# The last output projection of an RWKV5 and SwiGLU kernel: four of its thirds done unit by unit, stores of whole rows

## The chip, the cores and the metric

The kernel runs on one core of a Trainium2 chip. The metric is the device time of one execution in microseconds (us). The median of three runs before the change is 592.14 us (592.13 to 592.17).

## The reference

Two stages. The first is a linear attention with a decaying state (4 batches, 8 heads, 768 steps, head size 48); the second is a SwiGLU feed-forward block over the 3072 rows that come out of it.

```python
for t in range(S):
    cur = np.einsum('bhd,bhe->bhde', u[None] * kt, vt)
    y[:, :, t] = np.einsum('bhd,bhde->bhe', rt, state + cur)
    state = w[None, :, :, None] * state + np.einsum('bhd,bhe->bhde', kt, vt)
x = y.transpose(0, 2, 1, 3).reshape(B * S, H * D)      # 3072 x 384
g = x @ w_gate                                          # 384 x 1536
out = (g * (1.0 / (1.0 + np.exp(-g))) * (x @ w_val)) @ w_out   # 1536 x 384
```

All of it is in 32-bit floats. The change concerns only the last product, hidden values times `w_out`, for the last rows.

## The kernel before, in words

The 3072 rows are 24 blocks of 128 rows. Two blocks make a group for the feed-forward block, and from group 2 on two groups are worked on as a pair. A pair has two *units*, q = 0 and 1, with two blocks each, j = 0 and 1; so a pair puts out four blocks of 128 rows x 384 columns, 192 KB each. All engine orders are written out by hand: the program is a list of small pieces, and each engine does its instructions in the order in which the pieces issue them.

The output projections of the last two pairs use a product of matrices cut into thirds that takes 15 part products instead of 18. The function `project_thirds(g)` gives 15 pieces, one for each part product; here they are called *items* and go by the names r0 to r14 in the list `THIRDS`. An item multiplies a sum of hidden values by a sum of weights: for both units, four matmuls of 128x128x128 each, which are 16 matmul instructions on TensorE (PE). The result goes to a PSUM bank. Items of one *chain* (l1, l2, l8, n, y, l4, l5) add up in the same bank, and after each item the bank is evicted: copied, added or subtracted into one or two of the six output tiles c0 to c5 in SBUF, as the table `used` says. Copies are done by ScalarE (ACT), additions and subtractions by VectorE (DVE). Tile c[k] holds, for both units, 128 columns: block j = k % 2, third k // 2.

The items stand in this order; the second name is the chain:

```python
("r3", "l1"), ("r1", "l2"), ("r4", "l1"), ("r0", "l2"), ("r8", "l8"),
("r10", "n"), ("r14", "y"), ("r12", "l4"), ("r13", "n"), ("r2", "y"), ("r6", "l5"),
("r9", "l4"), ("r5", "n"), ("r11", "y"), ("r7", "l5"),
```

Before an item, `make(n)` may build sums of hidden values on DVE (line 999) that later items need. For the very last pair the flag `ends` is set.

PSUM has eight banks here: four in the queue `free` (the names bank0 to bank3) and four in `ring_a` (ring0 to ring3). A chain's first item takes a bank from the front of `free`; when the last item of a chain (`lasts`) has been evicted, the bank goes to the end of `free`. In the last projection chain l5 is *split*: it takes a second bank from `ring_a`, so that each unit has a bank of its own and is evicted as soon as its half of the item is done. The other chains hold both units in one bank, side by side, and are evicted for both at once with instructions of 128x256.

A block's row is whole when its three tiles are: block j = 0 with r9, r5 and r11, block j = 1 with r5, r11 and r7. So after r11 the blocks j = 0 of both units are stored in whole, and with `ends` also the first two thirds of the blocks j = 1 (128 KB each); the last third follows after r7 (64 KB each). Stores of unit 0 are issued by SyncE (SP), those of unit 1 by ACT, on the two engines' DMA queues q1 and q10. That makes six stores at the end of the kernel. For the pair before (`ends` not set) there are four whole stores, all issued by ACT.

The lines concerned: 999 (sums of hidden values), 1020 and 1022 (evictions by copy and by sum), 1027 (matmuls), 995 (stores); 944 to 951 prepare operands on GpSimd (POOL). After the last piece every engine takes a branch over a general version of the kernel that isn't run here (line 1381), and SP waits for all DMA semaphores.

Of the kernel before, what the change touches and what calls it, by code (L numbers as in the profile page):

```python
# [15 lines left out]
P = 128  # L16
# [6 lines left out]
def fast(  # L23
# [32 lines left out]
    DM, DFF = moe_w_gate.shape  # L56
# [8 lines left out]
    dve, pool, act, pe, sp = nc.vector, nc.gpsimd, nc.scalar, nc.tensor, nc.sync  # L65
# [23 lines left out]
    free = deque(banks[:2])  # L89

    ring_a = deque(ps_a.tile([P, 4 * P], FP32, name=f"ring{n}") for n in range(4))
# [6 lines left out]
    def take():  # L98
        return free.popleft()
# [178 lines left out]
    for e in range(2):  # L278
# [3 lines left out]
        out=u_row, in_=bass.AP(tensor=u.tensor, offset=u.offset, ap=[[0, 1], [1, H * D]]),  # L282
# [9 lines left out]
    def warm(n, bank=None):  # L292
# [14 lines left out]
        out=mask[:], in_=mask[:], compare_op=ALU.is_gt, fill=0.0,  # L307
# [11 lines left out]
    for l in range(7):  # L319
        n = 1 << l  # L320
# [451 lines left out]
    def prepare_threes(g, n):  # L772
        if n == 6:
            x_forms(g)
        for _ in range(2):
            if todo_x:
                todo_x.popleft()()
        if g > THREES:
            return
        if n == 1:  # L780
            if g == FIRST:
                todo_forms.extend(in_place(0) + in_place(1))
            if g == THREES:
                todo_forms.extend(w_forms(g, 1))
        if n == 7:
            todo_forms.extendleft(reversed(w_forms(g, 0)))
        for _ in range(2):
            if todo_forms:
                todo_forms.popleft()()
# [127 lines left out]
    def third(x, k, j):  # L917

        return x[:, :, 4 * k : 4 * k + 4, P * j : P * j + P]
# [39 lines left out]
    def project_thirds(g):  # L959

        ends = g + 2 == N // 2
        A, B_, C, D_, E, F = room["h"]
        (x00, x01), (x10, x11), (x20, x21) = (
            [third(hTs, k, j) for j in range(2)] for k in range(3)
        )
        h = {
            "r3": A, "r4": B_, "r1": C, "r0": D_, "r8": E, "r10": F, "r14": A, "r13": B_,
            "r12": C, "r2": D_, "r6": E, "r5": x00, "r7": x21, "r9": x20, "r11": x11,
        }
        rows = hv[:, NR + 6 : NR + 12].rearrange("p (q r) t -> p q (r t)", q=2)  # L970
        c = [rows[:, :, DM * (k % 2) + P * (k // 2) :][:, :, 0:P] for k in range(6)]
        made = {
            0: [(dve.tensor_sub, E, x01, x11)],
            1: [(dve.tensor_add, F, x01, x21)],
            2: [(dve.tensor_add, A, x10, x20)],
            3: [(dve.tensor_sub, B_, x00, F)],
            4: [(dve.tensor_add, C, B_, x20)],
            5: [(dve.tensor_sub, D_[q], D_[q], x20[:, q]) for q in range(2)],
            6: [(dve.tensor_add, E[:, q], D_[q], x21[:, q]) for q in range(2)],
        }  # L980
        used = {
            "r3": [("copy", 2)], "r4": [("copy", 1)], "r1": [("copy", 0)], "r0": [("sub", 2)],
            "r8": [("copy", 3), ("sub", 1)], "r10": [("copy", 5)], "r14": [("copy", 4)],
            "r12": [("add", 0)], "r13": [("add", 4)], "r2": [("add", 5)], "r6": [("add", 3)],
            "r9": [("sub", 4)], "r5": [("sub", 0), ("sub", 1)], "r11": [("add", 2), ("add", 3)],
            "r7": [("add", 5)],
        }
        lasts = ("r4", "r0", "r8", "r9", "r5", "r11", "r7")
        open_ = {}

        def store(q, j, a=0, z=DM):
            cc, b = divmod(2 * (g + q) + j, B)
            n0 = S * b + P * cc
            issue = sp if ends and q == 0 else act
            issue.dma_start(out=out[n0 : n0 + P, a:z], in_=rows[:, q, DM * j + a : DM * j + z])

        def make(n):
            for op, o, a, b in made.get(n, ()):
                op(o, a, b)
            if not ends:  # L1000
                prepare_threes(g + 2, n)

        def item(n):
            what, chain = THIRDS[n]
            if n:
                make(n)
            first = chain not in open_
            split = ends and chain == "l5"
            if first:
                open_[chain] = [take()] + ([ring_a.popleft()] if split else [])  # L1010
            banks_ = open_[chain]

            def evict(q):
                for how, k in used[what]:
                    x = banks_[0][:, 0 : 2 * P].rearrange("p (q t) -> p q t", q=2)
                    if split:
                        x = banks_[q][:, q * P : q * P + P]
                    o = c[k][:, q] if split else c[k]
                    if how == "copy":
                        act.copy(o, x)  # L1020
                    else:
                        (dve.tensor_add if how == "add" else dve.tensor_sub)(o, o, x)

            for q in range(2):
                ps = banks_[q if split else 0][:, q * P : q * P + P]
                for f in range(4):
                    pe.matmul(  # L1027
                        ps, (h[what][q] if h[what] is D_ else h[what][:, q])[:, f, :], wide["o"][what][:, f, :],
                        start=first and f == 0 and (split or q == 0), stop=f == 3, skip_group_check=True,
                    )  # L1030
                if split:
                    evict(q)
                    if what == "r7":
                        store(q, 1, 2 * P)
            if not split:
                evict(None)
            if n == 0:
                for do in wide.pop("last"):
                    do()
                make(0)  # L1040
            if what in lasts:
                free.append(banks_[0])
            if what == "r11":
                store(0, 0)
                store(1, 0)
                if ends:
                    store(0, 1, 0, 2 * P)
                    store(1, 1, 0, 2 * P)
            if what == "r7" and not ends:
                store(0, 1)  # L1050
                store(1, 1)
        return [lambda n=n: item(n) for n in range(15)]

    def three_units(g):
# [226 lines left out]
    for s in range(4, N + 2):  # L1281
# [3 lines left out]
        if s + 2 == SWAPPED:  # L1285
# [3 lines left out]
            for p, o in ((slice(0, 64), 64), (slice(64, P), -64)):  # L1289
                sp.dma_start(  # L1290
                    out=halves_of[p], in_=scales[p.start + o : p.stop + o, 1:3, H // 2 : H]
# [65 lines left out]
    ])  # L1357
    threes = three_units(THREES), three_units(THREES + 2)
    projections = project_thirds(THREES), project_thirds(THREES + 2)
    tail = threes[0] + projections[0][:-2]  # L1360
    tail += threes[1][0:1] + projections[0][-2:-1] + threes[1][1:2] + projections[0][-1:]
    tail += threes[1][2:] + projections[1]
    n = nc.values_load(outside, min_val=0, max_val=512)
# [416 lines left out]
```

## Time and profile before

| what | value |
|---|---|
| median of three runs | 592.14 us |
| the profiled execution | 591.4 us |
| its span | 589.7 us |
| PE busy | 578.3 us, 98% of the span |
| DVE busy | 421.0 us, 71% |
| ACT busy | 225.6 us, 38% |
| POOL busy | 355.5 us, 60% |
| granted TensorE clock | full in all 40 slices |
| stores at the end | 6: two of 192 KB, two of 128 KB, two of 64 KB |

The times in the traces are counted from the start of the span of one profiled execution. A line of the timeline gives start, duration, engine, source line, operation, and output <- inputs; "PEld" is TensorE's weight load, which runs beside its matmuls, and "SPq" and "ACTq" are the issuing of DMAs by these engines, not the transfer itself. The chain of waits is the work that ended last, followed back from the end. "To landing" is the time from a DMA's issue until its semaphore is complete.

### The profile page before, as it was taken

The numbers are of one execution on the slowest core, as the hardware profiler recorded it, in microseconds if no ns is written. First come the engines' busy times: TensorE is split into PE (matmuls) and PEld (weight loads), VectorE is DVE, ScalarE is ACT, GpSimd is POOL, SyncE is SP. The second block draws the span as 40 slices with busy tenths as digits, with TensorE's granted clock in tenths as the row PEclk, the third lists the DMA queues.
The fourth block names the chain that finished last, engine by engine and source line by source line (L and its number), as shares of the span: only waits on it lengthen the run. The fifth ranks groups of instructions, "written<-read, shape, count | busy, mean of one in ns | idle before, by whom it ended". The sixth has DMA issues, their size and how long they took to land.

```text
span 589.7 us, 13188 instructions
## 1 busy us (share of the span) xinstructions
PE 578.3 (98%) x5210; PEld 519.7 (88%) x5210; DVE 421.0 (71%) x703; ACT 225.6 (38%) x517; POOL 355.5 (60%) x378
## 2 busy tenths in 40 slices
PE   8999999999999999999999999999999999999996
PEld 7778888899888899988899988899988899888896
DVE  7788786479588776577887477779257877377672
ACT  4478885322343512245332345432134320233310
POOL 6899888989999403887501997422778960010610
PEclk9999999999999999999999999999999999999999
DMA  8989969432442323233244233200100000100001
GB/s 201 230 223 261 292 217 91 74 65 49 76 74 37 57 40 75 48 66 53 38 64 88 51 61 52 46 9 2 54 2 0 2 1 1 55 0 1 1 1 57
DMA packets 148292, 41.48 MB, mean 70 GB/s; under 512 B 138497, under 2 KB 142082, under 8 KB 148226
## 3 DMA queue, kind: packets, MB, share of 16 engines
q1 hardware_dynamic: 144914, 36.27, 30.4%
q10 hardware_dynamic: 3312, 4.33, 2.0%
q8 instruction: 42, 0.69, 0.5%
q14 instruction: 24, 0.20, 0.1%
HBM read 28.31 MB, written 4.72 MB: 56 GB/s over the span
## 4 chain that ended last, share of the span: by engine, by line
PE 93%; DVE 1%; ACT 0%; issue 0%; DVEq 0%; ACTq 0%
PE bank L801 31%; PE bank L620 18%; PE ring L801 13%; PE bank L545 10%; PE bank L1027 9%; PE ring L507 6%; PE ring L454 3%; PE ring L522 1%; PE ring L385 1%; DVE hv L825 0%; PE ring L1027 0%; DVE hs L594 0%; ACT At L364 0%; DVE hs L593 0%; DVE At L464 0%
## 5 line engine op out<-in xcount | busy, mean ns | idle before, releaser
L825 DVE TENSOR_TENSOR hv<-hv,bank 128x512 f32<-128x512 f32 x132 | 87.3, 681 | 26.3 <-PE bank L801 15.2
L545 PE MATMUL bank<-xT,wgv 128*128 128x256 f32 x288 | 66.2, 384 | 0.0
L801 PE MATMUL bank<-xf,wgv 128*128 128x256 f32 x256 | 65.9, 382 | 0.0
L364 ACT ACTIVATE At<-ident,du 128x128 f32<-128x128 f32 x176 | 59.9, 398 | 15.8 <-DVE du L265 8.9
L825 ACT COPY hv<-bank 128x512 f32<-128x512 f32 x72 | 40.1, 585 | 57.8 <-PE bank L801 51.4
L545 PEld LDWEIGHTS bank<-xT,wgv 128*128 128x128 f32 x288 | 53.4, 190 | 7.9
L731 POOL TENSOR_TENSOR s<-wgv 128x256 f32<-128x256 f32 x39 | 29.9, 790 | 48.6 <-PE bank L620 48.4
L801 PEld LDWEIGHTS bank<-xf,wgv 128*128 128x128 f32 x256 | 47.8, 190 | 7.0 <-DVE kT L1072 0.6
L1081 POOL TENSOR_TENSOR hv<-At,hats 128x512 f32<-128x512 f32 x8 | 10.2, 1277 | 66.3 <-ACT At L1080 66.3
L535 POOL TENSOR_TENSOR Z<-Z,w 48x192 f32<-48x192 f32 x32 | 16.8, 526 | 36.8 <-DVE Z L534 35.6
L507 PE MATMUL ring<-At,v_ld 128*32 128x128 f32 x768 | 35.6, 273 | 3.4 <-DVE At L464 2.5
L832 ACT ACTIVATE hv<-hv 128x512 f32<-128x512 f32 (+1 forms) x33 | 21.2, 668 | 45.4 <-DVE hv L825 45.3
L801 PE MATMUL bank<-xT,wgv 128*128 128x256 f32 x144 | 35.9, 382 | 0.0
L801 PE MATMUL bank<-xT,s 128*128 128x256 f32 x152 | 35.2, 380 | 0.0
L507 PEld LDWEIGHTS ring<-At,v_ld 128*32 128x32 f32 x768 | 30.5, 110 | 5.0 <-DVE At L464 4.5
L620 PE MATMUL bank<-wt,hs 128*128 128x192 f32 x192 | 33.7, 328 | 0.6 <-DVE hs L594 0.6
L620 PE MATMUL bank<-wo,hs 128*128 128x192 f32 x192 | 33.9, 327 | 0.0
L620 PE MATMUL bank<-wo,hv 128*128 128x192 f32 x192 | 33.4, 327 | 0.0
L801 PEld LDWEIGHTS bank<-xT,s 128*128 128x128 f32 x152 | 28.6, 190 | 4.5 <-issue 0.6
L620 PEld LDWEIGHTS bank<-wt,hs 128*128 128x128 f32 x192 | 31.3, 190 | 1.4 <-ACT At L364 0.8
L620 PEld LDWEIGHTS bank<-wo,hv 128*128 128x128 f32 x192 | 31.6, 190 | 0.4
L620 PEld LDWEIGHTS bank<-wo,hs 128*128 128x128 f32 x192 | 31.6, 190 | 0.3
(224 smaller groups left out, 1394.6 us busy)
## 6 DMA issues: line engine op xcount, KB each, us to landing
hats<-hats SPq DMA_DIRECT2D x192, 32.0 KB, 2.0
w_bits<-in_moe_w_gate_dram SPq DMA_DIRECT2D x6, 768.0 KB, 6.2
w_bits<-in_moe_w_val_dram SPq DMA_DIRECT2D x6, 768.0 KB, 6.2
w_bits<-in_moe_w_out_dram SPq DMA_DIRECT2D x6, 768.0 KB, 7.0
out_dram<-hv ACTq DMA_DIRECT2D x21, 192.0 KB, 1.9
v_ld<-in_v_dram SPq DMA_DIRECT2D x24, 96.0 KB, 5.5
k_ld<-in_k_dram SPq DMA_DIRECT2D x8, 192.0 KB, 4.3
r_ld<-in_r_dram SPq DMA_DIRECT2D x8, 192.0 KB, 4.4
```

What stands on the lines that cost most here:

```text
L364: lambda h=h: act.activation(At[i % 2][:, h, :], ident[:], AF.Identity, scale=du[:, h : h + 1])
L454: pe.matmul(ps[e][keys, a, cols], kT[i % 2][rows, at(i, a), keys], turned[i][rows, at(i, a), cols], start=True, stop=True, skip_group_chec ...
L507: pe.matmul(ps[32 * q : 32 * q + 32, cc, :], *x, start=start, stop=stop, skip_group_check=True,)
L535: pool.tensor_mul(ze, ze, w)
L545: pe.matmul(gv[:, o, :].rearrange("p (i t) -> p i t", i=2), wt[:, c, P * f : P * (f + 1)], xT[:, 2 * g % NX : 2 * g % NX + 2, c, :], start ...
L620: pe.matmul(ps, lhs[:, f, :], rhs[:, f, :], start=(f == 0 and n in (0, 1, 4)), stop=(f == FH - 1), skip_group_check=True,)
L731: op(made[o], made[a], made[b])
L801: pe.matmul(ps[:, o], u[:, o], v, start=first and o == 0, stop=True, skip_group_check=True,)
L825: do(out, *(pair_of(wide[a][:]) if isinstance(a, str) else a for a in args))
L832: todo.append((at, lambda: act.activation(gate, gate, AF.Silu)))
L1027: pe.matmul(ps, (h[what][q] if h[what] is D_ else h[what][:, q])[:, f, :], wide["o"][what][:, f, :], start=first and f == 0 and (split or ...
L1081: todo.append((muls, lambda: on.tensor_mul(h, sg, value)))
```

## The change

In the last pair the four last items (r9, r5, r11, r7) are done for unit 0 and then for unit 1, where they were done for both units each. For that, all four chains that these items belong to (n, y, l4, l5) are split: each unit has a bank of its own and evictions of 128x128. Both banks are taken when the chain opens, from `free`, or from `ring_a` when `free` is empty, and aren't given back. The six stores become four of whole rows: block 0 of a unit after its r11, block 1 after its r7. SP issues those of block 0 and ACT those of block 1. Other pairs are as before.

```diff
-        def store(q, j, a=0, z=DM):
+        def store(q, j):
...
-            issue = sp if ends and q == 0 else act
-            issue.dma_start(out=out[n0 : n0 + P, a:z], in_=rows[:, q, DM * j + a : DM * j + z])
+            issue = sp if ends and j == 0 else act
+            issue.dma_start(out=out[n0 : n0 + P, :], in_=rows[:, q, DM * j : DM * j + DM])
...
-        def item(n):
+        def item(n, halves=(0, 1)):
...
-            split = ends and chain == "l5"
+            split = ends and chain in ("n", "y", "l4", "l5")
             if first:
-                open_[chain] = [take()] + ([ring_a.popleft()] if split else [])
+                open_[chain] = [(free or ring_a).popleft() for _ in range(2 if split else 1)]
...
-            for q in range(2):
+            for q in halves:
...
                 if split:
                     evict(q)
-                    if what == "r7":
-                        store(q, 1, 2 * P)
+                    if what in ("r11", "r7"):
+                        store(q, what == "r7")
...
-            if what in lasts:
+            if what in lasts and not split:
                 free.append(banks_[0])
-            if what == "r11":
+            if what == "r11" and not ends:
                 store(0, 0)
                 store(1, 0)
-                if ends:
-                    store(0, 1, 0, 2 * P)
-                    store(1, 1, 0, 2 * P)
             if what == "r7" and not ends:
                 store(0, 1)
                 store(1, 1)
+        if ends:
+            pieces = [lambda n=n: item(n) for n in range(11)]
+            return pieces + [lambda n=n, q=q: item(n, (q,)) for q in range(2) for n in range(11, 15)]
         return [lambda n=n: item(n) for n in range(15)]
```

## The prediction

> **What bounds the kernel now.** I read the page's engine shares and chain first, then the chain and the timeline of the last 15 us, then every store issue, then the closing waits.
>
> ```profile
> PE 93%; DVE 1%; ACT 0%; issue 0%; DVEq 0%; ACTq 0%
> ...
> 574.90 1.23 PE bank L1027 x11
> 576.13 0.89 PE ring L1027 x8
> 577.03 6.25 PE bank L1027 x56
> 583.28 0.91 PE ring L1027 x8
> 584.19 0.02 issue
> 584.21 0.29 DVE hv L1022
> ```
>
> The columns of the chain are start, length, engine and line. The reader is to see that matmuls set the pace without a gap until 584.19 us, and that the last compute is one eviction, ending at 584.50. The span ends at 589.676: **5.18 us hold no compute**. The change touches that tail; the matmuls before it stay the same in number.
>
> The tail begins with six stores (start, length, queue):
>
> ```profile
> 582.87 0.37 SPq L995 DMA_DIRECT2D out_dram<-hv  x1
> 582.88 0.36 ACTq L995 DMA_DIRECT2D out_dram<-hv  x1
> 583.27 1.62 ACTq L995 DMA_DIRECT2D out_dram<-hv  x1
> 583.36 1.54 SPq L995 DMA_DIRECT2D out_dram<-hv  x1
> 584.93 0.46 ACTq L995 DMA_DIRECT2D out_dram<-hv  x1
> 584.99 0.41 SPq L995 DMA_DIRECT2D out_dram<-hv  x1
> ```
>
> The first pair issues in 0.37 us each, the second takes 1.6 us, and so the last pair, of 64 KB each, issues at 584.93 and 584.99, although the data was ready at 584.50 and 583.60. By the page the last ACT store lands 2.8 us after its issue, 587.73.
>
> Why 1.6 us? The trace's DMA packet records, which the views only sum, hold a 16 KB packet of the instruction queue q8 from 583.196 to 584.492, on one DMA engine. Both long issues end at 584.893 and 584.900, 0.40 us after that packet. The same holds earlier: at 324.523 to 325.470 there is such a packet, and
>
> ```profile
> 324.38 1.49 SPq L148 DMA_DIRECT2D v_ld<-in_v_dram  x1
> ```
>
> ends at 325.87, 0.40 us later. More than twenty issues follow this rule (0.3 to 0.5 us after the packet). Those that pass are the first one or two small ones: at 346.3 an issue of 128 descriptors that began 0.05 us before such a packet, with another one 0.7 us ahead of it, passed in 0.63, and the next was held. In the tail two stores of 128 descriptors passed and the third and fourth were held.
>
> After the landings come SyncE's closing waits:
>
> ```profile
> L1381 SPq EVENT_SEMAPHORE  x8: 17/17/17, 587.8 to 588.3; - x8
> L1775 SPq EVENT_SEMAPHORE  x10: 17/28/28, 588.4 to 589.6; - x10
> ```
>
> These eight are one wait per DMA semaphore, in the order of their numbers (101 to 108 in the trace), some 0.075 us apart. The last ACT store holds 101, the first in that order: it is released at 587.772, 0.04 us after the landing, and seven waits still follow (0.59 us to 588.366), then 1.31 us to the end. Release to end: 1.904 us.
>
> [...] PE's branch stands at 582.02 and the packet at 583.196; DVE's at 584.225 and an 8 KB packet of q14 at 585.443; ACT's and SP's at 585.42 and 585.45 and two at 586.83 and 586.87. [...]
>
> **The change part by part.**
>
> *Matmuls.* An item (one of 15 thirds) is 16 matmul instructions at 0.1117 us each, 1.787 us, half for each unit. The last four keep their 64 instructions; only their order changes to r9, r5, r11, r7 of unit 0, then of unit 1. Cost 0. The second halves use banks of their own, opened earlier, so nothing waits between them.
>
> *Evictions.* Eight DVE evictions of 128x256 (0.417 us) become sixteen of 128x128 (0.286), and two ACT copies of 0.37 become four halves: DVE gains 16 x 0.286 - 8 x 0.417 = 1.24 us. DVE waits for matmuls 1.0 to 1.5 us in each late item, which hides it: a half item lasts 0.893 us and brings at most two evictions. Without that cover it would cost up to 1.24 us.
>
> *Banks.* This is the new wait. With four free banks in order a, b, c, d (worked out from the code), l1 takes a, l2 b, l8 c; they return as a, b, c. Before, n took d, y a, l4 b, l5 c. Now n takes d and a, **y takes b and c**, l4 and l5 the four ring banks. So y's second half, at r14, needs c back from l8. The releaser is l8's subtraction, late in DVE's queue behind the sums of L999:
>
> ```profile
> 567.24 1.22 DVE L999 TENSOR_TENSOR hv<-hs,hv 128x1024 f32<-128x1024 f32 x1
> 567.93 1.50 PE L1027 MATMUL bank<-wo,hs 128*128 128x128 f32 x12
> 568.38 0.41 DVE L1022 TENSOR_TENSOR hv<-hv,bank 128x256 f32<-128x256 f32 x1
> ```
>
> It ends at 568.79. r14's weight loads start at 567.82, the second half's at 567.82 + 0.893 = 568.71. DVE to a waiting weight load took 0.054 us four times in this trace, so the load starts at 568.85: a stall of 0.13 us. Bounds: nothing, if the load doesn't wait, and 2.5 us, if DVE's four following sums (568.71 to 571.19) must end too. I take 0.13. Everything behind it, to the end, shifts by that; no slack follows on PE. b is free at 567.32, in time.
>
> *Stores.* Two of unit 0 leave some 3.5 us earlier (r11 and r7 of unit 0 end near 579.7 and 580.6) and are landed when the others come. Unit 1's: r11's first eviction begins where an eviction of the same kind began before, 583.317, ends at 583.60, and SP issues 0.027 us later (as 582.846 to 582.873), 583.63; with the stall 583.76. It falls into PE's fetch (583.33 to 584.62 shifted), but as the first with none ahead, so it passes in 0.37. Its data starts 0.85 us after issue (that of lone ACT stores), 584.61, just as the fetch ends. The last: r7 ends as before, eviction to 584.498, ACT issue 584.525, with the stall **584.655**; nothing queued ahead of it on ACT. Before, that was 584.933, held by the 1.6 us issue. Gain 0.28 us, though it is 192 KB instead of 64.
>
> *Landing.* Sixteen lone 192 KB stores:
>
> ```profile
> DMA to landing us min/median/max: 1.9/1.9/2.4
> ```
>
> In the records the last semaphore packet comes 1.52 us after issue. The unit's other store has moved its data by then (584.61 to 585.28; this one's 585.50 to 586.17). Before, 384 KB of four stores shared 585.4 to 586.65, and one engine trailed to 587.23. What remains is DVE's own 8 KB fetch, now near 585.57: 0.31 us alone on one engine, which every store uses too. I take it as fully paid: last semaphore 584.655 + 1.52 + 0.31 = 586.485. Bounds: 0 and 0.62 (SP's fetch, 1.42 us after its branch, falls at the same time and may share the engine). Semaphore to release: 0.42 for the lone ones, 0.54 in the old tail; I take 0.50, so 586.985.
>
> *Closing.* Semaphores have gone round in program order. Four stores now take 104 to 107, the last one 107; SP passes 101 to 106 while it lands. Left are two steps of 0.067 and the 1.31 us: 1.443, not 1.904.
>
> *Sum.* 586.985 + 1.443 = 588.43 against 589.676: 1.25 us less. The profiled execution took 591.4 with its 589.7 span, the median of the runs is 592.14; I take the tail to be the same in both: 592.14 - 1.25 = 590.89, **590.9**.
>
> **The rivals.**
>
> A, the forecast, 590.9, its own range 590.4 (no stall, no fetch in the way: 0.44 less) to 591.3 (second fetch and slow release). Chance 0.75.
>
> B, the fetch still holds the stores: SP's issue at 583.76 is kept to 584.62 + 0.40 = 585.02, both stores move together from 585.5. The first pair moved 384 KB in 1.1 us, so 586.6, + 0.31 + 0.50 + 1.443 = 588.85: 0.82 less, **591.3**. For it: twenty-odd held issues. Against: none of the held ones had nothing ahead of it. 0.10.
>
> C, the closing waits don't shorten, as the last store gets a number that is waited for first: 586.985 + 1.904 = 588.89, 0.79 less, **591.35**. Against: strict round robin in the last ten issues but for pairs swapped in place. 0.08.
>
> D, slower: the stall at r14's second half. If the wait takes in DVE's four sums up to 571.19, PE stands 571.19 + 0.05 - 568.71 = 2.53 us, 2.40 more than I count: **593.3**. It decides from a stall of 1.25 + 0.13 = 1.4 us on. For it: DVE is busy without a break from 562.4 to 571.2, and any wait there lands on PE at once. Against: waits in this trace are met 0.05 us after the one instruction they name. 0.07.
>
> **How the numbers follow.** Some 0.2%, 1.18 us, is what a measurement of this kernel can tell from no change, and the forecast stands just beyond. Of A's 0.75, 0.54 lies beyond 1.18 us (a second fetch or a slow release takes it under); B, C and the rest of A are "same", and D is split. Faster 0.54, same 0.41, slower 0.05. Range 590.3 to 591.8: A with its bounds, B and C.
>
> **What would show it.** Right: four stores, none longer than 0.5 us; the last on ACT at 584.6 to 584.7; a PE gap of 0.1 to 0.2 us at L1027 near 568.8; the last of the eight waits reached soon after the last landing, and 1.45 us from there to the end. Wrong: an issue of over 1 us at 583.8 (B), seven waits after the last landing (C), a gap of microseconds after 568.7 (D), or a last landing more than 2.6 us after its issue.

## The result and the profile after

The median of 22 runs is 591.64 us, against 592.28 us for the kernel before in the same runs. The ratio is 0.9987, with a 95% interval of 0.9981 to 0.9993: a gain of 0.13%, some 0.77 us (the two medians lie 0.64 us apart). The profiled execution took 591.58 us, with a span of 589.85.

The single times scatter by more than the change is worth (591.0 to 592.6 after, 591.8 to 595.1 before). So most readings below are made within one trace, from the start of the last eviction to the end of the span. I call that stretch the **tail**. It was 5.47 us before.

The page's engine shares and the chain of waits of the changed kernel:

```profile
PE 91%; POOL 3%; DVE 2%; SPq 2%; issue 1%; ACT 0%; DMA 0%; POOLq 0%; DVEq 0%; ACTq 0%
...
580.60 1.79 PE ring L1027 x16
582.39 1.79 PE bank L1027 x16
584.17 0.91 PE ring L1027 x8
585.08 0.02 issue
585.11 0.29 DVE hv L1022
```

Matmuls still run until the last eviction, in the new order of banks, and the eviction starts at 585.106 instead of 584.210. So this execution was 0.90 us late at that point, but only 0.13 us of that arose in the last projection. Its first weight load starts at 557.77 instead of 557.00, before any changed instruction: the rest comes from the program in front, whose time differs from trace to trace.

The four stores in the timeline of the changed kernel (start, length, queue):

```profile
581.00 0.37 SPq L995 DMA_DIRECT2D out_dram<-hv  x1
581.91 0.34 ACTq L995 DMA_DIRECT2D out_dram<-hv  x1
584.53 0.35 SPq L995 DMA_DIRECT2D out_dram<-hv  x1
585.42 0.34 ACTq L995 DMA_DIRECT2D out_dram<-hv  x1
```

None is held: they take 0.34 to 0.37 us. The last issues 0.32 us after the start of the last eviction (0.72 before). SP's at 584.53 begins 0.09 us before the 16 KB packet that follows PE's branch (584.615 to 585.560) and passes. In the repeat of this kernel ("changed, again" below) the same store begins 0.15 us inside that packet (583.899 to 584.845) and passes too:

```profile
584.04 0.35 SPq L995 DMA_DIRECT2D out_dram<-hv  x1
```

SyncE's waits in the changed kernel, the landing of its ACT stores, and the last ACT store of the kernel before, whose last figure is the time to landing:

```profile
L1381 SPq EVENT_SEMAPHORE  x8: 17/17/17, 585.5 to 588.5; - x8
```

```profile
DMA to landing us min/median/max: 1.9/1.9/3.0
```

```profile
out_dram<-hv ACTq DMA_DIRECT2D x1, 64.0 KB, 2.8
```

SP starts its eight waits at 585.5. It stands at the sixth, for the third store, until 586.998, and at the seventh, for the last store, until 588.406. From there to the end it takes 1.444 us (1.904 before). But the last store lands **3.0 us** after its issue, later than the 64 KB store did.

The end of that transfer in stretches (stretch, length, busy time of PE, PEld, DVE, ACT and POOL with counts, PE clock, DMA share, GB/s):

```profile
585.20:586.20 1.00, 0.00 (x0) 0.00 (x0) 0.19 (x1) 0.00 (x0) 0.00 (x0) 1.00 0.56 200
586.20:587.00 0.80, 0.00 (x0) 0.00 (x0) 0.00 (x0) 0.00 (x0) 0.00 (x0) 1.00 0.69 255
587.00:587.95 0.95, 0.00 (x0) 0.00 (x0) 0.00 (x0) 0.00 (x0) 0.00 (x0) 1.00 0.07 15
```

In the third stretch the DMA share is 0.07, about one engine of sixteen. The packet records agree: the last store left 128 packets of 1536 bytes and sixteen of 4 bytes, which I read as the semaphore packet of each engine's part; of these sixteen, fourteen are done by 586.94, one at 587.09 and the last at 587.93. By that reading one engine works for nearly another microsecond; SP's wait for this store ends only at 588.406, 0.48 us after that last packet.

### The profile page after: what moved, and what is told of

Its sections match the earlier page's. It is cut to its first block, busy times and chain, and to the rows that moved or that the text cites. A ratio compares the mean times of both kernels' runs of the same rounds, so it can differ in the third digit from the quotient of the medians.

```text
span 589.9 us, 13199 instructions
## 1 busy us (share of the span) xinstructions
PE 579.3 (98%) x5210; PEld 519.9 (88%) x5210; DVE 424.1 (72%) x711; ACT 226.4 (38%) x519; POOL 355.8 (60%) x378
## 4 chain that ended last, share of the span: by engine, by line
PE 91%; POOL 3%; DVE 2%; SPq 2%; issue 1%; ACT 0%; DMA 0%; POOLq 0%; DVEq 0%; ACTq 0%
PE bank L801 28%; PE bank L620 18%; PE ring L801 13%; PE bank L545 10%; PE bank L1027 8%; PE ring L507 6%; PE ring L454 3%; SPq L411 2%; PE ring L385 1%; POOL s L731 1%; PE ring L1027 1%; PE ring L522 1%; PE ring L296 1%; DVE At L464 1%; DVE hv L825 0%
```

## The experiments

The tail is split into three terms: from the start of the last eviction to the last ACT issue; from there until SP is released by the last landing; and from there to the end. "Gap" is the pause in the last projection's weight loads. An "instruction packet" (a "fetch" in the prediction) is a DMA record of q8 or q14, which the page lists with the kind `instruction`. At the end of the changed kernel there are four: one of q8, 16 KB, 1.70 us after PE's branch (582.916), and three of q14, 8 KB each, at 586.164, 586.752 and 586.961, which are 1.24, 1.63 and 1.17 us after the branches of SP (584.929), DVE (585.121) and ACT (585.791). They are named after these engines; which branch a packet of q14 belongs to is taken from their order. All in us:

| kernel | gap | to issue | to release | to end | tail | ratio to before (95%) |
|---|---|---|---|---|---|---|
| before | 0 | 0.72 | 2.84 | 1.90 | 5.47 | 1 |
| changed | 0.13 | 0.32 | 2.98 | 1.44 | 4.74 | 0.9987 (0.9981 to 0.9993) |
| changed, again | 0.13 | 0.32 | 3.04 | 1.44 | 4.80 | 0.9990 (0.9983 to 0.9997) |
| before, no branch | 0 | 0.32 | 2.04 | 1.30 | 3.65 | 0.9969 (0.9959 to 0.9980) |
| changed, no branch | 0.13 | 0.32 | 1.88 | 0.93 | 3.12 | 0.9975 (0.9962 to 0.9987) |
| changed, other banks | 0 | 0.32 | 3.07 | 1.44 | 4.83 | 0.9991 (0.9981 to 1.0001) |
| stores only | 0 | 0.32 | 3.50 | 1.51 | 5.33 | 0.9994 (0.9985 to 1.0003) |
| order only | 0.12 | 0.59 | 2.59 | 1.90 | 5.08 | 1.0003 (0.9994 to 1.0012) |
| changed, queues by unit | 0.13 | 0.38 | 2.86 | 1.44 | 4.68 | 0.9993 (0.9985 to 1.0002) |
| changed, DVE late | 0.12 | 0.32 | 2.16 | 1.44 | 3.92 | 0.9979 (0.9972 to 0.9987) |
| all three | 0 | 0.37 | 1.88 | 1.44 | 3.70 | 0.9972 (0.9960 to 0.9983) |
| all three, again | 0 | 0.37 | 1.88 | 1.44 | 3.70 | 0.9968 (0.9960 to 0.9977) |
| before, DVE late | 0 | 0.58 | 2.22 | 1.90 | 4.71 | 0.9987 (0.9980 to 0.9994) |

Tail and gap together foretell the timed ratio: all three, 3.70 - 5.47 = -1.77 us, 0.30%, against 0.28 and 0.32% timed; changed, 4.74 + 0.13 - 5.47 = -0.60 us, 0.10%, against 0.13 and 0.10%.

### Is it the instruction packets? Both kernels without the branch

```diff
-    n = fast(tc, *args, outside[:])
-    with tc.If(n > 0, label="general"):
-        general(tc, *args)
+    fast(tc, *args, outside[:])
...
-    tc.mark_branch_hint_location("general", engines=list(mybir.ALL_ENGINES))
```

> The kernel before without the branch over the general version at its end (the version for other decay rates is left out; with these inputs it isn't run anyway). In the kernel before, the last eviction starts at 584.21 us and the span ends 5.47 us later. Theory F [...]: without the branch there is no 16 KB packet of q8 near the stores, so no store issue is longer than 0.5 us, the last stores issue as soon as their data is there (some 0.31 us after the start of the last eviction), and the tail shrinks from 5.47 to about 4.0 us: 1.2 to 1.6 us faster than before. Theory S (the stores themselves are slow: six in a row with short rows on two queues): the second pair is still held for some 1.5 us, and the tail stays within 0.3 us of 5.47.

> The changed kernel without the branch and the general version. Its tail is 4.74 us from the start of the last eviction (585.106) to the end of the span, and its last store landed some 2.94 us after its issue. Theory F: the last landing falls to 1.9 to 2.1 us after its issue, as for a lone store, and the tail to 3.7 to 4.0 us. Theory S (192 KB simply land late behind another 192 KB): landing 2.7 us or more, tail 4.5 us or more. If F holds for both kernels without the branch, the change is worth little between them: 0.1 to 0.4 us.

With the branch, its closing waits go too, so the first two terms of the tail are what this edit tells. The stores of the kernel before without the branch, in its timeline:

```profile
584.98 0.47 ACTq L995 DMA_DIRECT2D out_dram<-hv  x1
585.06 0.38 SPq L995 DMA_DIRECT2D out_dram<-hv  x1
585.53 0.51 SPq L995 DMA_DIRECT2D out_dram<-hv  x1
586.24 0.34 ACTq L995 DMA_DIRECT2D out_dram<-hv  x1
```

The second pair, held for 1.6 us before, now passes in 0.47 and 0.38: the six stores in a row were not the cause. The landings of the ACT stores in the changed kernel without the branch:

```profile
DMA to landing us min/median/max: 1.9/1.9/2.0
```

Not 3.0 any more: here 192 KB behind another 192 KB landed like a lone store (1.9). What theory F said of the issues and of the landing held (the longest issue took 0.51 us), and no instruction packet appears in the last 9 us of either trace. Its sizes were too small: the tails fell to 3.65 and 3.12 us, below the forecast 4.0 and 3.7 to 4.0, since without the branch the closing is shorter as well (1.30 and 0.93 us; SP's eight separate waits are gone). Between the two kernels the change is worth 0.53 us of tail less the gap of 0.13, about 0.4 us; the timed intervals are too wide to tell them apart.

### The gap: other banks

```diff
-                open_[chain] = [(free or ring_a).popleft() for _ in range(2 if split else 1)]
+                open_[chain] = [take()] + ([ring_a.popleft()] if split else [])
```

> The changed kernel, with the second bank of each split chain from the ring, so that y's second half doesn't get l8's bank. The gap of 0.13 us in front of the second half of r14's weight loads goes (244 ns between two loads there, 112 elsewhere), everything after it comes 0.13 us earlier; the time falls by 0.1 to 0.2 us against the changed kernel, which is less than the runs scatter. Rival: the gap is something else and stays.

The place in the timeline of the changed kernel:

```profile
569.04 1.10 PEld L1027 LDWEIGHTS bank<-wo,hs 128*128 128x128 f32 x8
569.15 0.42 DVE L1022 TENSOR_TENSOR hv<-hv,bank 128x256 f32<-128x256 f32 x1
```

and with the other banks:

```profile
569.95 0.97 PEld L1027 LDWEIGHTS ring<-wo,hs 128*128 128x128 f32 x8
```

Eight loads take 1.10 us in one and 0.97 in the other. In the changed kernel the second half's first load comes 0.244 us after the one before it, 0.052 after the end of DVE's subtraction from l8's bank (569.563). With a ring bank the step is 0.112, as elsewhere in that projection. From the first to the last weight load the projection takes 26.917 us in the changed kernel, 26.791 with the other banks and in the kernel before. The gap is real and worth 0.126 us; the timed ratio can't show that.

### Either half of the change alone

Stores only, on the kernel before: its order and banks, but whole rows.

```diff
                     if what == "r7":
-                        store(q, 1, 2 * P)
+                        store(q, 1)
...
-                if ends:
-                    store(0, 1, 0, 2 * P)
-                    store(1, 1, 0, 2 * P)
```

> The kernel before with its order and banks, but four stores of whole rows: block 0 of both units after r11, block 1 of a unit after its half of r7. Theory F: the first pair issues in 0.37 us; of the second pair the one of SP is ready near 583.63, inside the 16 KB packet that followed PE's branch, and as the third in a row it is held until 0.4 us after that packet, 584.9; ACT's follows at once. Data of both moves from 585.4, tail 4.9 to 5.3 us, 0.2 to 0.6 us faster than before. Theory O (the gain comes from whole rows and fewer stores alone): the tail is that of the changed kernel, 4.7 us or less.

```profile
584.44 1.22 SPq L995 DMA_DIRECT2D out_dram<-hv  x1
```

This is SP's second store in that kernel's timeline. PE's packet lies at 583.969 to 585.265, and the issue ends at 585.667, 0.40 us after it, as in the kernel before (0.40 and 0.41). This held store is the one that lands last and sets the release of 3.50 in the table. The tail is 5.33, just above theory F's range; theory O is out.

Order only, on the changed kernel: six stores again, three for each unit.

```diff
-                    if what in ("r11", "r7"):
-                        store(q, what == "r7")
+                    if what == "r11":
+                        store(q, 0)
+                        store(q, 1, 0, 2 * P)
+                    if what == "r7":
+                        store(q, 1, 2 * P)
```

> The changed order and banks, but the stores cut as before: after a unit's r11 block 0 whole and two thirds of block 1, after its r7 the last third, 64 KB; unit 0 by SP, unit 1 by ACT. Theory F: unit 0's three are through long before. Of unit 1's, the first two issue on ACT in a row at 584.4, in PE's 16 KB packet, as the first two in it, so they pass in 0.34 and 0.45 us, and the last follows its eviction at once, if the packet is over; if it is held, until 0.4 us after the packet. It moves 64 KB instead of 192, and ends the tail at 4.4 to 4.9 us, as the one lagging engine sets it and not the size. Theory W (whole rows matter): the tail is back at 5.2 us or more.

The tail is 5.08 us, outside theory F's range and short of theory W's. Two terms explain it. The second issue on ACT was expected to pass, but it takes 0.63 us, until 0.39 us after PE's packet (585.986 to 587.171), and puts the last one off (0.59 instead of 0.32). And with six stores the last one holds semaphore 101 again, so the closing is 1.90 us:

```profile
586.93 0.63 ACTq L995 DMA_DIRECT2D out_dram<-hv  x1
```

So neither half brings the gain by itself. In the traces each saves 0.1 to 0.3 us, which the timed ratios don't tell from nothing. The order gets unit 0's stores out before PE's packet, the smaller number of stores shifts the last semaphore, and only both together leave that packet a single store to meet.

### Whose packet makes the last engine lag?

Queues by unit, then DVE's branch late:

```diff
-            issue = sp if ends and j == 0 else act
+            issue = sp if ends and q == 0 else act
```

> The changed kernel with the stores shared out by unit: SP issues both of unit 0, ACT both of unit 1. Where the changed kernel ends, one DMA engine does its eight packets of the last store only after the others are done (587.06 to 587.92, the others until 586.95), beside three 8 KB instruction packets that follow the branches of SP (586.164), DVE (586.752) and ACT (586.961). Here SP takes its branch some 3 us earlier, so its packet is gone from there. Theory SP (that packet, ahead of the store on the one engine, starts the lag): the last store is released 1.9 to 2.3 us after its issue, tail 3.8 to 4.1 us instead of 4.74. Theory DVE (it is DVE's packet that the engine does first): the release stays 2.7 to 3.1 us after issue and the tail within 0.3 us of 4.74.

```diff
         if ends:
             pieces = [lambda n=n: item(n) for n in range(11)]
-            return pieces + [lambda n=n, q=q: item(n, (q,)) for q in range(2) for n in range(11, 15)]
+            def late():
+                dve.tensor_add(A, x10, x20)
+                dve.tensor_add(A[:, 0, 0], x10[:, 0, 0], x20[:, 0, 0])
+            return pieces + [lambda n=n, q=q: item(n, (q,)) for q in range(2) for n in range(11, 15)] + [late]
```

> The changed kernel with two more additions on DVE after its last eviction (128x1024 and 128x128, into a buffer that nobody reads any more), which put DVE's branch, and so its instruction packet, 1.3 us later, behind the last store. Theory DVE: the lag of the one engine goes, release 1.9 to 2.3 us after issue, tail 3.7 to 4.1 us instead of 4.74, some 0.6 to 1.0 us faster than the changed kernel. Theory SP: the lag stays, release 2.7 to 3.1 us after issue, tail 4.5 to 4.9. A tail longer than 4.9 us would show that the additions themselves hold up SP's closing waits.

With SP's branch 2.6 us earlier the release moves from 2.98 to 2.86 us only (DVE's packet takes 0.77 us in that trace, not 0.31). With DVE's branch later it falls to 2.16: 0.82 us. Theory DVE held in both. The end of the kernel with DVE late, in its timeline:

```profile
585.74 0.29 DVE L1022 TENSOR_TENSOR hv<-hv,ring 128x128 f32<-128x128 f32 x1 [0.41 <-PE ring L1027]
585.95 1.22 DVE L1052 TENSOR_TENSOR hs<-hv 128x1024 f32<-128x1024 f32 x1
586.06 0.34 ACTq L995 DMA_DIRECT2D out_dram<-hv  x1
587.20 0.29 DVE L1053 TENSOR_TENSOR hs<-hv 128x128 f32<-128x128 f32 x1
```

Two useless additions (L1052 and L1053) make the kernel faster: DVE's branch comes at 587.214 instead of some 0.02 us after the start of the last eviction, and its packet at 588.431, after the store's last data (587.73).

The three edits together:

> The changed kernel with the banks of the run without the gap, the stores by unit and DVE's branch late. With either theory no instruction packet but ACT's own is left near the last store, and that one comes 1.2 us after ACT's branch, when the data is through: release 1.9 to 2.1 us after issue, tail 3.7 to 3.9 us, and the time 0.9 to 1.3 us below the changed kernel, 1.5 to 2.0 below the kernel before. If the lag has another cause than these packets, the tail stays above 4.4 us.

> The version with the other banks, the stores by unit and DVE's branch late, once more: from its traces' terms 0.13 (gap) and 1.1 us (release 1.88 instead of 2.98 us after the issue), so 1.0 to 1.3 us below the changed kernel and 0.25 to 0.35% below before. If the gain over the changed kernel is under 0.5 us, the terms of one trace don't carry over to the timed runs.

The landings of the ACT stores in the second of the two runs, and the last stretches of that transfer:

```profile
DMA to landing us min/median/max: 1.9/1.9/2.0
```

```profile
586.50:587.25 0.75, 0.00 (x0) 0.00 (x0) 0.56 (x2) 0.00 (x0) 0.00 (x0) 1.00 0.73 273
587.25:587.60 0.35, 0.00 (x0) 0.00 (x0) 0.00 (x0) 0.00 (x0) 0.00 (x0) 1.00 0.00 0
```

No engine lags. This version beats both kernels: 0.9968 (0.9960 to 0.9977) of the kernel before, and measured beside it the changed kernel stood at 0.9990 (0.9983 to 0.9997):

> The changed kernel once more, beside the two others of this call. From its first 22 runs: 0.1 to 0.2% below before. In the trace: the gap in front of r14's second half again 0.12 to 0.13 us, the last store released 2.7 to 3.1 us after its issue, 1.44 us from there to the end.

Last, the same two additions on the kernel before:

> The kernel before with the same two late additions on DVE. If DVE's instruction packet holds up the last stores there too, the release of the last ACT store, 2.84 us after its issue in the kernel before, comes down to 2.1 to 2.4, and the end of the span, 4.74 us after that issue, to 4.0 to 4.3: 0.4 to 0.7 us faster than before. The held second pair stays, as PE's packet is still there. Rival: in the kernel before the queue of 384 KB sets the landing and not the packet; then nothing changes (within 0.2 us).

The landings of the ACT stores there lie between 1.9 and 3.5 us, and the last one's release falls from 2.84 to 2.22 us after its issue, although the second pair is still held (1.48 and 1.42 us). The tail falls by 0.76 us; the other 0.14 lie ahead of the last issue, as PE's packet ends 0.14 us earlier relative to the last eviction in that trace. These two lines alone gain as much on the kernel before, 0.13%, as the whole change.

## Why the prediction was nearly right, and where it was off

The direction was right, but the size was 0.60 us of tail and gap in the traces, where the sum said 1.25: half. Of the 0.60, the earlier issue brings 0.40 and the shorter closing 0.46; the later landing takes back 0.14 and the gap 0.13. The time, 591.64 us, lay inside the full range but outside the forecast's own, 590.4 to 591.3. The range reached 591.8 because it left room for rivals B and C, and neither came true; that the time fell into this room was luck. The gain also lies under the 1.18 us that the prediction thought measurable and held for more likely than not to be passed; 22 runs of each tell a smaller one from nothing.

- **Matmuls and evictions**: right. 26.791 us and the one gap; the added DVE work (1.24 us forecast, 1.26 in the traces) stays hidden.
- **Banks**: right. A stall of 0.13 us was forecast at the second half of r14; the traces show 0.12 to 0.13 in every kernel with these banks. Rival D is out.
- **Stores**: right. Four, none longer than 0.37 us; the last 0.32 us after the start of the last eviction, as worked out. Rival B is out, though in the changed kernel's own trace the store begins just before PE's packet, which came 1.70 us after PE's branch and not 1.18. The repeat decides it, and so do the traces with other banks and with DVE late: a first store that begins inside the packet passes in 0.35 us. That the held issues came from this packet, which the prediction had inferred from times alone, is now borne out by its removal (0.47 and 0.38 us instead of 1.62 and 1.54). How it holds them is not shown: the traces give only the two ends, 7 ns apart.
- **Closing**: right. 1.443 us forecast, 1.444 found. Rival C is out.
- **Landing: the step that failed.** The prediction put issue to release at 1.52 + 0.31 + 0.50 = 2.33 us, with DVE's packet counted at its own length, 0.31, and 2.64 at most. It is 2.98, and 3.04 in the repeat; the landing 3.0 us after the issue is the sign of being wrong that the prediction had named (more than 2.6). Of the three terms the 0.50 held (0.48); the last semaphore packet comes 2.51 us after the issue, where 1.52 + 0.31 = 1.83 was forecast. The term that was mis-sized is the 0.31 for the packet. The last store of the changed kernel without the branch, with no packet near it, was released after 1.88. So the packets cost 1.1 us, not the 0.45 that lies between 1.88 and 2.33. DVE's accounts for 0.82 of it; in the version with all three edits the other 0.28 is gone too. That is the whole error: 2.98 - 2.33 = 0.65, and 1.25 - 0.65 = 0.60.

The same step hid a second misreading. The old tail's trailing engine was seen (587.23 against 586.65) but put down to 384 KB in four stores, so a gain of 0.5 us was booked for their going. The kernel before with DVE late shows that 0.62 us of its landing was DVE's packet, which the change leaves where it was.

**What stays open.** Why a packet of 0.31 us costs 0.8. The records name no DMA engine, so that an instruction packet runs on an engine which the stores use too is my inference; the one part of sixteen that lags fits it. In all four traces with the changed stores, the branch and DVE's branch early (the kernel, its repeat, other banks, queues by unit), one engine begins its eight packets of the last store within 4 ns of the end of DVE's packet (587.063 and 587.066; 587.459 and 587.463), some 0.8 us after the others in the two whose times stand here. It then does two to four of them in 0.16 to 0.22 us each instead of 0.065. That DVE's packet holds them back on its engine would fit this. What slows the packets after it was not tried, but it isn't special to DVE's: after PE's packet, too, three packets of a store take 0.18, 0.23 and 0.13 us (before and changed kernel), and without the branch none of the last stores' packets does. ACT's packet runs at the same time as the lag (586.961 to 587.450), and its part was not separated. Nor was the part of SP's packet separated from that of the banks in the version with all three edits.

## What to carry to other kernels

In this kernel the branches of PE, SP, DVE and ACT at the end were each followed by an instruction packet 1.1 to 1.7 us later, and moving DVE's behind the last transfer saved 0.6 to 0.8 us of landing. Where a kernel ends in a branch, find in the DMA records whose packet falls there, and try to move that engine's end, even with idle work. Price such a packet by what an engine lags in the trace, not by its own length (here 0.82 us against 0.31). Where a tail ends in a list of waits, it also counts at which place of the list the last transfer stands: here the seventh place of eight, not the first, saved 0.46 us.

## What the runs showed that was not expected

- Two additions that nobody needs shorten the tail of both kernels by 0.8 us. In the changed kernel all of it comes from the later branch of DVE; in the kernel before 0.62 us do.
- The store issues that began inside PE's 16 KB packet behind others ended 0.40 us after that packet: they were 1.62, 1.54, 1.48, 1.42 and 1.22 us long in three kernels, and store issues took 0.34 to 0.51 without the packet. With the changed order and six stores the second issue in the packet ended 0.39 us after it.
- The code ahead of the last projection is the same in all these kernels (but for a hint for the branch in the two without it), and yet its first weight load starts anywhere from 557.0 to 559.7 us in their traces. A change of 0.1% is better read in the trace of its own stretch than in the total.
